# Loads, weight sums and query fills moved, and the last product cut in two, in a TensorE-bound transformer block

## The chip, the cores and the metric

The kernel runs on one core of a Trainium2 chip. The metric is the time of one execution on the device, in microseconds (us). Each kernel was run several times, in rounds together with the kernel before on the same chip; one run of each was also recorded by the hardware profiler. PE is the TensorE, DVE the VectorE, ACT the ScalarE, SP the engine that issues most DMAs. A "hole" below is a stretch in which PE starts no matmul.

## The reference

For x of 2048 rows and 1024 columns (bf16), in short:

```python
def A(x):                              # linear attention, 32 heads of 32
    q, k, v = split(x @ wqkv)
    pq, pk = phi(q), phi(k)            # phi(t) = t+1 if t > 0 else exp(t); plus 1e-6
    kv = einsum("bhsd,bhse->bhde", pk, v);  z = sum_s pk
    return ((pq @ kv) / (pq . z + 1e-6)) @ wo
def B(x):                              # MLP over the rows, F = 3584
    u = gelu(layernorm(x).T @ w1 + b1)
    return (u @ w2 + b2).T
h  = x + A(layernorm(x))
h2 = h + B(layernorm(h))
```

## The kernel before

The program has four stretches: a head, in which rows of x are normalised, transposed and multiplied by the key weights, tile by tile (a tile is 128 rows; "unit (i,c)" is tile i times key or value block c of 512 columns); the V and K runs, in which key and value projections of two tiles at a time are done with seven instead of eight block products (Strassen's scheme in Winograd's form, parts p1 to p7); attention; and the MLP, again with seven products (m1 to m7). Query projections ("fills") are put between parts of the runs where PE would wait.

The loads of the head: the first block of the key weights goes in two halves on the queue of ACT, all else on that of SP.

```python
xs = {0: load_x(0, True)}              # x0 in two halves, one on each queue
for k0 in (0, hk):
    pin(nc.scalar.dma_start(wkv[:, k0:k0+hk, 0:CW], wqkv_v[:, k0:k0+hk, D:D+CW]))   # key block 1
for i in range(1, 4):
    xs[i] = load_x(i)
for c in range(1, 2 * NDC):            # key block 2, value blocks 1 and 2
    nc.sync.dma_start(wkv[:, :, c*CW:(c+1)*CW], wqkv_v[:, :, D+c*CW:D+(c+1)*CW])
    ...                                # x4, x5; later the query weights
```

The end of the head and the first V run. `pin` keeps program order on an engine. `ln_stats` is DVE work (statistics of a tile); `ln_finish` is Ln and Exp on ACT, a normalisation on DVE and a transposing DMA. `w_sums` and `x_sums` are DVE work: four sums of 1.2 us (128x2048), four of 0.42 us (128x512). A fill is eight matmuls, then Exp and Relu on ACT and two DVE instructions.

```python
proj_unit(3, 0, pin)
ln_stats(G0)                           # G0 = 4
proj_unit(2, 1, pin)
load_biases(trp)
ln_finish(G0)
proj_unit(3, 1, pin)
...                                    # value units of tiles 0 and 1, w_sums(vmov, ..), x_sums(1)
v1 = VRun(1)
v1.p1(); q_fill(); kv_accum(0); kv_accum(1)
v1.p6(); v1.p2()
w_sums(kmov, 0)
q_fill()
ln_stats(G0 + 2)
v1.p5()
q_fill()
ln_finish(G0 + 2)
load_next(2 * G0)
v1.p7()
w_sums(kmov, 1)
q_fill()
x_sums(2)
...                                    # K run 2: p1, (p3, p4 of v1), p6, ...
```

In a run, p1 makes `psA` and ACT copies it to `psB`; p6 accumulates into `psB`, which lies in one of two PSUM slots that the fills use too. While `psB` lives there is one slot for fills, so a fill waits until the Relu of the fill before has read its slot.

The last product of the MLP, and the way its result leaves:

```python
def evac(sh, dh, ps):                  # DVE, then the store
    nc.vector.scalar_tensor_tensor(ot[sh][:, c], ps[:], b2_sb[...], hr[sh][:, c], ALU.add, ALU.add)
    nc.sync.dma_start(o_dram[...], ot[sh][:, c])
def m7(self):
    self.mm(7, self.X, False, True)    # 14 matmuls of 128x512
    self.evac(0, 0, self.X)
...
pend.m7()                              # end of the program
```

## Time and profile before

Before: 581.24 us, median of 3 runs (581.16 to 581.6). The profiled run was the one of 581.6 us.

| | value | view |
|---|---|---|
| span | 579.9 us | page |
| PE busy | 569.9 us, 98% | page |
| start to start of 128x512 matmuls, everywhere but in the warm-up | 0.216 us | timeline |
| waits of PE, all listed | 4.9 us | waits |
| start of the last product to the end | 6.9 us | timeline |

The chain of waits of the kernel before, by engine (first line of that part of the page):

```profile
PE 96%; DMA 1%; DVE 1%; ACT 0%; issue 0%; ACTq 0%; DVEq 0%
```

Who PE waited for in the kernel before (total us, times, longest):

```profile
PE acc_t L422 <- DMA wkv<-in_A_wqkv_dram: 2.0, 2, 1.3
PE acc_t L93 <- DVE warm L85: 1.2, 1, 1.2
PE psB L498 <- DVE xs L484: 0.9, 1, 0.9
PE acc_t L753 <- ACT r_sb L161: 0.6, 2, 0.3
PE tp L666 <- DVE xn L401: 0.2, 1, 0.2
```

So a change of order can win at most some 4 us, and a part of the tail. Where the waits lie, from the timeline of PE (start, length, what; in brackets the idle time and what ended it). The length of a matmul group includes the drain of the last one, so a hole is better read from start to start.

```profile
7.93 1.02 PE L422 MATMUL acc_t<-wkv,xnT 128*128 128x512 bf16 x4 [1.34 <-DMA wkv<-in_A_wqkv_dram]
8.96 0.72 PE L666 MATMUL tp<-ident,xn 128*128 128x128 bf16 x8
10.39 2.75 PE L422 MATMUL acc_t<-wkv,xnT 128*128 128x512 bf16 x12 [0.70 <-DMA wkv<-in_A_wqkv_dram]
...
34.91 1.02 PE L498 MATMUL psB<-wo_sb,xs 128*128 128x512 f16 x4
...
39.70 1.89 PE L753 MATMUL acc_t<-xnT,wq_sb 128*128 128x512 bf16 x8 [0.31 <-ACT r_sb L161]
41.42 1.03 PE L498 MATMUL psC<-wo_sb,xs 128*128 128x512 f16 x4
42.76 1.89 PE L753 MATMUL acc_t<-xnT,wq_sb 128*128 128x512 bf16 x7 [0.31 <-ACT r_sb L161]
...
48.15 1.04 PE L498 MATMUL psB<-pqT,xs 128*128 128x512 f16 x4 [0.92 <-DVE xs L484]
...
572.97 3.19 PE L228 MATMUL psX<-gO,sa 128*128 128x512 f16 x14
```

The first and the third line begin with the two halves of unit (0,0), which wait for the two halves of the key weights; the second is the transposes of tile 1. The line at 34.91 is p6 of the first V run. The two at 39.70 and 42.76 are fills that wait for the Relu (`r_sb`) of the fill before. The one at 48.15 is p6 of K run 2, which waits for its x sums. The last is the last product.

### The profile page before, as it was taken

The page shows a single profiled execution, that of the slowest core. Times are in us where ns is not written, and L with a number is a line of the kernel's source. Part 1 is how long each engine was busy: PE and PEld are TensorE (multiplying, and loading weights), DVE is VectorE, ACT ScalarE, POOL GpSimd, SP SyncE. Part 2 cuts the span into 40 slices and gives each one's busy share as a digit, 9 for nine tenths or more (in the row PEclk, how much of TensorE's full clock was granted, in tenths as well). Part 3 has the DMA queues.
Part 4 walks back from the last instruction along what each step waited for, and adds up shares of the span by engine and source line. Part 5 has one row for each costly group of instructions (what it writes and reads, how often), then busy time and mean ns, then how long its engine had stood idle before and what let it go on. Part 6 is the DMA issues. An engine that isn't in the chain of part 4 may idle for free.

```text
span 579.9 us, 7451 instructions
## 1 busy us (share of the span) xinstructions
PE 569.9 (98%) x2817; PEld 266.4 (46%) x2840; DVE 386.0 (67%) x751; ACT 212.5 (37%) x432; POOL 1.8 (0%) x8
## 2 busy tenths in 40 slices
PE   7999999999999999999999999999999999999997
PEld 3444444454555444444444444444444444444443
DVE  6788888546667889876666766667765456456542
ACT  4756777765667777342222322223000000000000
POOL 1000000000000000000000000000000000000000
PEclk9999999999999999999999999999999999999999
DMA  9933333019637952152224322203966446531101
GB/s 304 353 69 74 73 74 55 19 44 316 96 73 152 292 174 92 56 145 72 73 72 118 100 74 72 73 0 96 226 205 162 125 114 172 137 90 46 36 28 36
DMA packets 109667, 66.55 MB, mean 115 GB/s; under 512 B 31666, under 2 KB 101568, under 8 KB 109632
## 3 DMA queue, kind: packets, MB, share of 16 engines
q1 hardware_dynamic: 108368, 64.89, 42.7%
q10 hardware_dynamic: 1200, 1.18, 0.6%
q8 instruction: 22, 0.36, 0.3%
q14 instruction: 13, 0.11, 0.1%
q0 software_dynamic: 64, 0.01, 0.0%
HBM read 50.34 MB, written 8.39 MB: 101 GB/s over the span
## 4 chain that ended last, share of the span: by engine, by line
PE 96%; DMA 1%; DVE 1%; ACT 0%; issue 0%; ACTq 0%; DVEq 0%
PE psX L228 17%; PE psZ L228 17%; PE psW L228 17%; PE acc_t L902 9%; PE acc_t L753 9%; PE psY L228 8%; PE psB L498 4%; PE psA L498 4%; PE psC L498 4%; PE acc_t L422 3%; PE psE L498 2%; DMA wkv<-in_A_wqkv_dram 1%; PE nd_ps L853 1%; PE kvps_462 L451 1%; PE kvps_463 L451 0%; DVE pqT L472 0%
## 5 line engine op out<-in xcount | busy, mean ns | idle before, releaser
L228 PEld LDWEIGHTS <-sa 128*128 128x128 f16 x1120 | 109.6, 98 | 132.2
L223 DVE TENSOR_TENSOR sa<-w1p 128x1024 f16<-128x1024 bf16 x70 | 48.0, 685 | 20.0 <-PE psX L228 12.4
L753 PE MATMUL acc_t<-xnT,wq_sb 128*128 128x512 bf16 x247 | 57.4, 379 | 1.0 <-ACT r_sb L161 0.6
L902 PE MATMUL acc_t<-wo_sb,pqT 128*128 128x512 bf16 x250 | 55.7, 379 | 0.3
L223 DVE TENSOR_TENSOR sa<-w2p 128x1792 f16<-128x1792 bf16 x40 | 43.4, 1084 | 10.1 <-PE psW L228 7.6
L902 PEld LDWEIGHTS <-pqT 128*128 128x128 bf16 x256 | 24.8, 98 | 29.0
L753 PEld LDWEIGHTS <-wq_sb 128*128 128x128 bf16 x256 | 24.5, 98 | 28.4 <-issue 1.2
L164 DVE TENSOR_SCALAR e_sb<-e_sb 128x512 bf16<-128x512 bf16 x64 | 18.5, 290 | 27.3 <-ACT e_sb L160 26.7
L264 DVE TENSOR_TENSOR tt<-psW,dd 128x512 f32<-128x512 f32 x22 | 15.2, 692 | 29.2 <-PE psW L228 29.2
L228 PEld LDWEIGHTS <-w1p 128*128 128x128 bf16 x224 | 21.9, 98 | 26.4
L228 PEld LDWEIGHTS <-w2p 128*128 128x128 bf16 x224 | 21.9, 98 | 26.4
L160 ACT ACTIVATE e_sb<-acc_t 128x512 bf16<-128x512 f32 x40 | 23.9, 599 | 26.9 <-PE acc_t L753 23.7
L259 DVE TENSOR_TENSOR psY<-psX,dd 128x512 f32<-128x512 f32 x22 | 15.4, 699 | 27.5 <-PE psX L228 27.5
L498 PEld LDWEIGHTS <-xs 128*128 128x128 f16 x208 | 20.0, 98 | 24.1 <-DVE xs L484 2.3
L269 DVE TENSOR_TENSOR tt<-tt,psZ 128x512 f32<-128x512 f32 x22 | 15.1, 688 | 18.0 <-PE psZ L228 17.9
L228 PE MATMUL psZ<-hT_2226,w1p 128*128 128x512 f16 x112 | 26.8, 379 | 0.0
L228 PE MATMUL psW<-hE,sa 128*128 128x512 f16 x112 | 26.6, 379 | 0.0
L228 PE MATMUL psX<-hT_2225,sa 128*128 128x512 f16 x112 | 26.6, 379 | 0.0
L498 PE MATMUL psA<-wkv,xnT 128*128 128x512 bf16 x99 | 26.3, 379 | 0.3
L228 PE MATMUL psZ<-hO,sa 128*128 128x512 f16 x112 | 26.5, 379 | 0.0
L228 PE MATMUL psW<-hT_2227,w1p 128*128 128x512 f16 x112 | 26.5, 379 | 0.0
L228 PE MATMUL psY<-hE,sa 128*128 128x512 f16 x112 | 26.5, 379 | 0.0
(256 smaller groups left out, 839.1 us busy)
## 6 DMA issues: line engine op xcount, KB each, us to landing
w1p<-in_B_w_dram SPq DMA_DIRECT2D x14, 1024.0 KB, 5.8
w2p<-in_B_w_dram SPq DMA_DIRECT2D x8, 1792.0 KB, 8.5
xr<-in_A_x_dram SPq DMA_DIRECT2D x16, 256.0 KB, 3.4
x_sb<-in_A_x_dram SPq DMA_DIRECT2D x15, 256.0 KB, 3.7
wkv<-in_A_wqkv_dram SPq DMA_DIRECT2D x3, 1024.0 KB, 10.4
wq_sb<-in_A_wqkv_dram SPq DMA_DIRECT2D x2, 1024.0 KB, 11.4
wo_sb<-in_A_wo_dram SPq DMA_DIRECT2D x2, 1024.0 KB, 6.6
wkv<-in_A_wqkv_dram ACTq DMA_DIRECT2D x2, 512.0 KB, 7.6
```

The costliest lines, as they stand in the source:

```text
L160: pin(nc.scalar.activation(e_sb[:], src, ACT.Exp))
L164: pin(nc.vector.tensor_scalar(e_sb[:], e_sb[:], 1.0, PHI_EPS, ALU.min, ALU.add))
L223: return nc.vector.tensor_tensor(t, a, b, op)
L228: nc.tensor.matmul(ps[:], lhsT=sa[:, k, :], rhs=mv(k), start=(start and k == 0), stop=(stop and k == self.nk - 1), skip_group_check=True,)
L259: nc.vector.tensor_tensor(self.Y[:], self.X[:], self.d[:], ALU.add)
L264: nc.vector.tensor_tensor(self.t[:], self.W[:], self.d[:], ALU.add)
L269: nc.vector.tensor_tensor(self.t[:], self.t[:], self.Z[:], ALU.subtract)
L422: mm = nc.tensor.matmul(pp[:, 0:CW], lhsT=xnT[:, kt, i * P:(i + 1) * P], rhs=wkv[:, kt, c * CW:(c + 1) * CW], start=(kt == 0), stop=(kt == ...
L451: pin(nc.tensor.matmul(kv_ps[b][:, sl, :], lhsT=pks[i % NPK][:, j * P:(j + 1) * P], rhs=vaugs[i % NVA][:, j, :], start=False, stop=(i == N ...
L498: pin(nc.tensor.matmul(ps[:], lhsT=lhs[:, k, :], rhs=rhs[:, k, :], start=(start and k == 0), stop=(k == hk2 - 1), skip_group_check=True,))
L753: nc.tensor.matmul(qp[:, 0:SW], lhsT=wq_sb[:, kt, j * P:(j + 1) * P], rhs=xnT[:, kt, u * SW:(u + 1) * SW], start=(kt == 0), stop=(kt == ND ...
L902: nc.tensor.matmul(ap_[:, 0:CW], lhsT=pqT[:, j, i * P:(i + 1) * P], rhs=wo_sb[:, j, dc * CW:(dc + 1) * CW], start=(j == 0 and not SEED_RES ...
```

## The change

Its intent: bring the key weights in before x2 and x3; do two of the four key weight sums early; put p5 and p7 between the fills, so that no fill waits, and make the x sums of run 2 early; cut the last product in two column parts (384 and 128), so that the store of the first runs under the second. The number of fills before K run 2 drops from four to three; the fourth moves to the end of the runs.

```diff
-        def evac(sh, dh, ps):
+        def evac(sh, dh, ps, a=0, b=CW):            # only columns a to b
...
-        def m7(self):
-            self.mm(7, self.X, False, True)
-            self.evac(0, 0, self.X)
+        def m7(self, cuts=(0, CW)):
+            for a, b in zip(cuts, cuts[1:]):
+                self.mm(7, self.X, False, True, cols=slice(a, b))
+                self.evac(0, 0, self.X, a, b)
...
             xs = {0: load_x(0, True)}
+            xs[1] = load_x(1)
             for k0 in (0, hk):
-                pin(nc.scalar.dma_start(wkv[:, k0:k0 + hk, 0:CW], wqkv_v[:, k0:k0 + hk, D:D + CW]))
+                nc.sync.dma_start(wkv[:, k0:k0 + hk, 0:CW], wqkv_v[:, k0:k0 + hk, D:D + CW])
...
-            for i in range(1, 4):
+            for i in range(2, 4):
                 xs[i] = load_x(i)
...
                 if i == 2:
                     phis[0][1]()
                     phis[1][1]()
+                    w_sums(kmov, slice(0, 1))
...
             proj_unit(3, 0, pin)
+            w_sums(kmov, slice(1, 2))
             ln_stats(G0)
...
             v1.p2()
-            w_sums(kmov, 0)
+            w_sums(kmov, slice(2, 4))
             q_fill()
+            x_sums(2)
             ln_stats(G0 + 2)
             v1.p5()
-            q_fill()
+            v1.p7()
             ln_finish(G0 + 2)
             load_next(2 * G0)
-            v1.p7()
-            w_sums(kmov, 1)
             q_fill()
-            x_sums(2)
...
-            for n in range(2):
+            for n in range(3):
                 q_fill()
...
-    pend.m7()
+    pend.m7((0, CW - P, CW))
```

More of the change, by code (lines that the diff above doesn't have):

```diff
@@ L188, in prefetch @@
                 ot.append(outp.tile([P, D], BF16, tag=f"ot{a}", name=f"ot{a}"))
-        def evac(sh, dh, ps):
+        def evac(sh, dh, ps, a=0, b=CW):
             i = 2 * p + sh
-            c = slice(dh * CW, (dh + 1) * CW)
-            nc.vector.scalar_tensor_tensor(ot[sh][:, c], ps[:], b2_sb[:, i:i + 1], hr[sh][:, c], ALU.add, ALU.add)
+            c = slice(dh * CW + a, dh * CW + b)
+            nc.vector.scalar_tensor_tensor(ot[sh][:, c], ps[:, a:b], b2_sb[:, i:i + 1], hr[sh][:, c], ALU.add, ALU.add)
             nc.sync.dma_start(o_dram[i * P:(i + 1) * P, c], ot[sh][:, c])
@@ L223, in asum, with mm @@
             return nc.vector.tensor_tensor(t, a, b, op)
-        def mm(self, m, ps, start, stop, ks=None):
+        def mm(self, m, ps, start, stop, ks=None, cols=slice(0, CW)):
             sa, mv = self.sa[m], self.mov[m]
@@ L228, in mm @@
                 nc.tensor.matmul(
-                    ps[:],
+                    ps[:, cols],
                     lhsT=sa[:, k, :],
-                    rhs=mv(k),
+                    rhs=mv(k)[:, cols],
                     start=(start and k == 0),
@@ L320, in w1_evac, with evac @@
     def w1_evac(p):
-        def evac(fh, dh, ps):
+        def evac(fh, dh, ps, *cut):
             dst = (gE if fh == 0 else gO)[:, p, dh * CW:(dh + 1) * CW]
@@ L470, in w_sums @@
                 (b11, b12, b21, b22), (t1, t2, t3, t4) = mov
-                for out, a, b in ((t1, b12, b11), (t2, b22, t1), (t3, b22, b12), (t4, b21, t2))[2 * part:2 * part + 2]:
+                for out, a, b in ((t1, b12, b11), (t2, b22, t1), (t3, b22, b12), (t4, b21, t2))[part]:
                     pin(nc.vector.tensor_tensor(out, a, b, ALU.subtract))
@@ L738 @@
             proj_unit(0, NDC, pin)
-            w_sums(vmov, 0)
+            w_sums(vmov, slice(0, 2))
             proj_unit(0, NDC + 1, pin)
@@ L742 @@
             proj_unit(1, NDC, pin)
-            w_sums(vmov, 1)
+            w_sums(vmov, slice(2, 4))
             proj_unit(1, NDC + 1, pin)
```

## The prediction

> **What bounds it now.** TensorE. The chain of waits is 96% PE, the page shows PE busy 98% of 579.9 us, and a 128x512 matmul starts every 0.216 us wherever PE runs. Only PE gaps and the tail can be won. The timeline shows them (start to start): 1.3 us at 6.6 us (first key unit waits for the key weights, queued on ACT); 0.7 us at 9.7 us (their second half, landing at 10.35); 0.48 us at 39.2 and at 42.3 us (each query fill waits until the fill before has freed its PSUM slot); 1.1 us at 47.1 us (K run 2 waits for its x sums, behind two 1.2 us key weight sums on DVE); 3.9 us after the last matmul.
>
> **Key weights behind x0, x1.** In the DMA records both queues share one stream of about 340 GB/s, so today x2 and x3 travel beside the key weights; the Trainium skill, "DMA: Bandwidth & Descriptors", section "Queues, rings and completion order", says too that an engine alternates between queues. Queued first, the halves should land near 6 and 8 us. The second transposes still wait for DVE (8.96 us), so the first hole only shifts; the second closes (0.7 us). Then unit (0,1) needs the next key block: last landing 13.03 us today, used at 13.42, its bytes not moved earlier. I expect a new DMA wait; net 0.25 us (0 to 0.7).
>
> **Key sums early.** Two 1.2 us sums enter DVE between 17 and 23 us, where it idles for little more than one of them; it is packed from 22.4 to 34.8 us. The first V run's s1, s2 end at 34.13, PE needs them at 34.91. DVE falls 1.1 us behind PE, the slack is 0.7: a new wait of 0.4 us at psB of the first V run.
>
> **Fills respaced.** p5 and p7 now stand between fills (1.73 us, against the 1.3 us that Exp and Relu need after one): both 0.48 us holes go, and the hole at the x sums too: 2.05 us. But ACT now meets Ln/Exp of tile 6, which stand before the third fill's Exp/Relu and K run 2's copy to psB, only after DVE finished x sums and statistics. From the end of fill 2 I sum 7.0 us of measured steps to K run 2's p6, against 6.0 us of PE work: a new hole of 1.0 us there. Net 1.05 us. The moved fill runs at the phase's end without a wait.
>
> **Last product in 384+128 columns.** Meant to overlap evacuation and store. But in the built program the second part's first matmul waits for the first part's evacuation: same PSUM bank. (The skill, "PSUM — Partial Sum Buffer", section "Terms", calls two engines in one bank at once an error; no run here shows it.) Estimate, from 129-column matmuls at 0.058 us and 0.75 us for a 512-column evacuation: 2.27 + 0.2 + 0.6 + 0.06 + 0.85 + 0.2 + 0.3 + 2.65 to the end = 7.1 us, against 6.93 now: 0.2 us lost.
>
> **Sum.** 0.25 - 0.4 + 1.05 - 0.2 = 0.7 us gained: 580.5 us, range 579.6 to 581.4. Faster by over 2%: 0.01; within 2%: 0.98; slower: 0.01.
>
> **Shows right or wrong:** no PE wait before the second half of unit (0,0); a DMA wait near 13 us; V run 1's p6 waiting for xs; no waits between fills; K run 2's p6 waiting for ACT; PE idle 0.9 us between the last product's parts.
>
> **Could be wrong:** key block 2 landing later; DVE's lag absorbed; a shorter ACT chain; a tail that gains.

## The result and the profile after

Changed kernel: 580.85 us, median of 6 runs (580.36 to 581.29); before: 581.25 us (581.16 to 581.6, 6 runs). The ratio of the fast runs is 0.9992, with a 95% interval of 0.9979 to 1.0005: the same. (Ratios in this text are the mean time of one kernel's fast runs over that of the other's of the same rounds, so not quite the ratio of the medians quoted.) The outputs are correct. In these rounds the runs of the changed kernel lie wider apart than those of before: 0.93 us against 0.44. In the later rounds the kernel before scattered as much or more (fast runs 580.89 to 582.54, 580.87 to 582.09 and 581.02 to 582.75 us), so a wider scatter of the changed kernel is not shown.

The profiled run took 580.46 us (span 578.7 us). Who PE waited for in the changed kernel (its line numbers are up to four higher):

```profile
PE tp L668 <- DVE xn L402: 2.0, 2, 1.0
PE acc_t L93 <- DVE warm L85: 1.2, 1, 1.2
PE psX L228 <- DVE ot_5119 L193: 0.7, 1, 0.7
PE psB L499 <- ACT psB L512: 0.5, 1, 0.5
PE acc_t L423 <- ACT r_sb L161: 0.4, 1, 0.4
PE acc_t L423 <- ACT xnT L678: 0.4, 1, 0.4
```

Of the old waits only the warm-up's and that of the transposes (`tp`, for DVE's normalisation) are left. The second is 2.0 us here and 0.2 above, and the one for `xnT` (0.4 us) is not in the list above; but a second trace of the kernel before, shown below, has both at the same 2.0 and 0.4 us, so the change did not bring them. The other three are new. The timeline of PE:

```profile
7.13 1.04 PE L423 MATMUL acc_t<-wkv,xnT 128*128 128x512 bf16 x4 [0.35 <-ACT xnT L678]
9.15 0.72 PE L668 MATMUL tp<-ident,xn 128*128 128x128 bf16 x8 [0.98 <-DVE xn L402]
9.71 2.75 PE L423 MATMUL acc_t<-wkv,xnT 128*128 128x512 bf16 x12
12.29 0.61 PE L668 MATMUL tp<-ident,xn 128*128 128x128 bf16 x8
12.79 3.61 PE L423 MATMUL acc_t<-wkv,xnT 128*128 128x512 bf16 x15
...
26.08 5.34 PE L423 MATMUL acc_t<-wkv,xnT 128*128 128x512 bf16 x24 [0.36 <-ACT r_sb L161]
...
34.79 1.02 PE L499 MATMUL psB<-wo_sb,xs 128*128 128x512 f16 x4
...
45.08 1.02 PE L499 MATMUL psB<-pqT,xs 128*128 128x512 f16 x4 [0.55 <-ACT psB L512]
...
571.61 2.44 PE L228 MATMUL psX<-gO,sa 128*128 128x384 f16 x14
574.76 0.94 PE L228 MATMUL psX<-gO,sa 128*128 128x128 f16 x14 [0.71 <-DVE ot_5119 L193]
```

The fills wait no more. The hole before p6 of K run 2 is now from 44.37 (four matmuls of 0.216 us after 43.51, where p4 starts) to 45.08, 0.7 us, ended by ACT's copy to `psB`. A new hole of 0.5 us stands before 26.08 us. And between the parts of the last product PE stands idle: 14 matmuls of 0.162 us (three quarters of 0.216) after 571.61 end at 573.88, the next starts at 574.76, 0.88 us later, when DVE has evacuated the first part.

The new hole at 26 us comes from DVE by way of ACT. The timeline of ACT in the changed kernel there:

```profile
22.56 0.59 ACT L161 ACTIVATE r_sb<-acc_t 128x512 bf16<-128x512 f32 x1
24.53 0.29 ACT L398 ACTIVATE lnv<-mv,eps_ln 128x1 f32<-128x1 f32 x1 [1.38 <-DVE mv L395]
24.86 0.20 ACT L399 ACTIVATE rstd<-lnv 128x1 f32<-128x1 f32 x1
24.96 0.58 ACT L160 ACTIVATE e_sb<-acc_t 128x512 bf16<-128x512 f32 x1
25.44 0.59 ACT L161 ACTIVATE r_sb<-acc_t 128x512 bf16<-128x512 f32 x1
```

ACT waits 1.38 us with Ln of tile 4 for the statistics (`mv`), which stand on DVE behind the second early key sum; the Exp and Relu of unit (3,1) stand behind it on ACT, although their data is there, and PE needs the PSUM slot that this Relu frees.

### The profile page after: what moved, and what is told of

It reads as the page before. It is cut to its first block, busy times and chain, and to the rows that moved or that the text cites. A ratio compares the mean times of both kernels' runs of the same rounds, so it can differ in the third digit from the quotient of the medians.

```text
span 578.7 us, 7486 instructions
## 1 busy us (share of the span) xinstructions
PE 569.4 (98%) x2832; PEld 267.2 (46%) x2854; DVE 385.7 (67%) x752; ACT 211.9 (37%) x432; POOL 1.8 (0%) x8
## 4 chain that ended last, share of the span: by engine, by line
PE 96%; DVE 2%; ACT 1%; issue 0%; DMA 0%
PE psX L228 17%; PE psW L228 17%; PE psZ L228 17%; PE acc_t L904 9%; PE acc_t L757 9%; PE psY L228 8%; PE psB L499 4%; PE psA L499 4%; PE psC L499 4%; PE acc_t L423 3%; PE psE L499 2%; PE nd_ps L855 1%; DVE st L392 1%; PE kvps_464 L452 1%; PE kvps_465 L452 0%
## 5 line engine op out<-in xcount | busy, mean ns | idle before, releaser
L228 PE MATMUL psX<-hO,sa 128*128 128x512 f16 x112 | 26.5, 379 | 0.0
```

The lines of the kernel that those rows point to most:

```text
L228: nc.tensor.matmul(ps[:, cols], lhsT=sa[:, k, :], rhs=mv(k)[:, cols], start=(start and k == 0), stop=(stop and k == self.nk - 1), skip_gro ...
```

## The experiments

Twelve kernels ran, one of them the kernel before again, all with correct outputs. They ran on two chips, so each is best compared by its ratio to the kernel before in the same rounds; the changed kernel has 0.9992. One run of the kernel before took 1877.52 us and counts as slow; it is in no ratio.

### The tail: last product whole

```diff
-    pend.m7((0, CW - P, CW))
+    pend.m7()
```

> The changed kernel with the last product in one piece again. My theory: the second part waits for the first part's evacuation, so the cut costs; without it the span after the start of the last product goes from 7.09 us back to about 6.93, and the time falls by 0.1 to 0.2 us. Rival, the intent of the cut: it hides most of an evacuation, so without it the time rises by 0.3 to 0.5 us.

Measured: 580.86 us (580.41 to 581.78, 5 runs), ratio to before 0.9992 (0.9979 to 1.0005). From the start of the last product to the end: 6.86 us in its trace, 7.07 in that of the changed kernel (571.61 to 578.68), 6.88 in that of before (572.97 to 579.86). The cut costs 0.2 us in the traces; the medians, with their scatter, don't resolve that. The rival's 0.3 to 0.5 us gain is ruled out by the traces.

### The tail: two PSUM banks

```diff
+            # last pair only: psX for columns 0..383, a second psX tile for 384..511;
+            # m1, the two DVE adds into psX, m7 and evac work on (tile, a, b) in turn
+        def m7(self):
+            for ps, a, b in self.parts():
+                self.mm(7, ps, False, True, cols=slice(a, b))
+                self.evac(0, 0, ps, a, b)
```

> The changed kernel, with the last pair's accumulator in two PSUM banks (384 and 128 columns), so that the second part need not wait for the evacuation of the first; the first product of that pair is cut in the same places. My theory (the shared bank makes the wait): no PE idle time between the two parts, and about 6.4 us from the start of the last product to the end instead of 7.09, so 0.6 us less than the changed kernel. Rival (128-column matmuls or the second small store are what costs): the tail stays within 0.2 us of 7.09.

Measured: 580.16 us (579.43 to 580.73), ratio 0.9978 (0.9965 to 0.9991). The tail takes 6.18 us, 0.9 less than in the changed kernel and 0.7 less than before. Its timeline of PE:

```profile
572.16 3.22 PE L230 MATMUL psX<-gO,sa 128*128 128x384 f16 x28
```

All 28 matmuls are one uninterrupted group: the 128-column part is no burden in itself. So the wait came with the shared bank, and the intent of the cut was sound and its form was not. (This version also makes two tiles of one; no run tells the shared tile from the shared bank.) The Trainium skill, "PSUM — Partial Sum Buffer", section "Terms", says that TensorE writing and VectorE reading one bank at once is an error; the built program accordingly had a wait for the evacuation at the first matmul of the second part, and no run here tried without.

### The loads: new order alone

```diff
# on the kernel before
+            xs[1] = load_x(1)
             for k0 in (0, hk):
-                pin(nc.scalar.dma_start(...))
+                nc.sync.dma_start(...)
-            for i in range(1, 4):
+            for i in range(2, 4):
```

> The kernel before with the new order of loads alone (key weights behind x0 and x1 on one queue). My theory: the wait of 0.7 us before the second half of unit (0,0) goes, PE runs 0.6 to 0.7 us earlier from there to the first V run, DVE has slack there, so the kernel is 0.4 to 0.7 us faster than before (580.5 to 580.9). Rival: the gain is taken back by x2 or key block 2 landing later, or by the x sums, and the time stays within 0.2 us of before.

Measured: 581.27 us (581.06 to 581.45), ratio 0.9999 (0.9985 to 1.0013). The rival was right: no gain.

### The kernel before, a second look

> The kernel before, unchanged, for a second trace. The first one came from a run of 581.6 us, 0.4 above the usual 581.2, and one of the 16 landings of every load after about 7 us came some 1.07 us after the other 15. My theory: that late engine differs from run to run, and the 0.7 us hole before the second half of unit (0,0), which the prediction counted as the prize of the new queue order, is largely the late engine's doing. Then a run near 581.1 shows last landings within 0.3 us of the 15th and a hole of 0.2 us or less there. Rival: the hole is that of the two queues sharing the engines, and it is again 0.6 to 0.8 us.

Measured: 580.92 us (one run), span 579.1 us. The timeline of PE in this second trace of the kernel before:

```profile
7.09 1.04 PE L422 MATMUL acc_t<-wkv,xnT 128*128 128x512 bf16 x4 [0.36 <-ACT xnT L676]
9.11 0.72 PE L666 MATMUL tp<-ident,xn 128*128 128x128 bf16 x8 [0.98 <-DVE xn L401]
9.66 2.75 PE L422 MATMUL acc_t<-wkv,xnT 128*128 128x512 bf16 x12
12.25 0.61 PE L666 MATMUL tp<-ident,xn 128*128 128x128 bf16 x8
12.70 1.67 PE L422 MATMUL acc_t<-wkv,xnT 128*128 128x512 bf16 x6
```

The two DMA waits of the first trace (1.34 and 0.70 us) are not there. They were not a property of the kernel but of that run. Every load is spread over 16 DMA engines and posts 16 landings; the time of the 15th and of the last, from the records of the traces (us):

```
                          before, 1st trace   before, 2nd trace   changed kernel
key block 1, 1st half       6.93 /  7.79        5.71 /  5.74        6.67 /  6.70
key block 1, 2nd half       9.52 / 10.35        9.30 /  9.32        8.38 /  8.39
key block 2                11.96 / 13.03       11.59 / 11.61       12.74 / 12.75
```

In the first trace one landing is 0.8 to 1.1 us behind the other 15. In the second it is not. The new order brings the second half in earlier (8.4 us), but PE cannot use it before 9.7 us, since it comes to it only after the second transposes, which wait for DVE. And it brings the first half and key block 2 in later by 1 us each. The first half now has x1 in front of it. Key block 2 has the same bytes in front of it in both orders; there the reason is the rate. Busy time of each engine and, last, the GB/s of all DMA between 5.0 and 6.5 us in the second trace of before, then in the trace with the new order alone:

```profile
5.00:6.50 1.50, 0.52 (x8) 0.39 (x8) 1.24 (x3) 0.53 (x3) 0.00 (x0) 1.00 1.08 381
```

```profile
5.00:6.50 1.50, 1.02 (x7) 0.28 (x6) 1.35 (x4) 0.50 (x2) 0.00 (x0) 1.00 0.76 238
```

In the four traces with the loads on two queues that stretch shows 342 to 381 GB/s; in the ten with one queue 181 to 351. Why the single queue is slow there was not tested.

### Key block 2 in two halves

```diff
             for c in range(1, 2 * NDC):
-                nc.sync.dma_start(wkv[:, :, ...], wqkv_v[:, :, ...])
+                # c == 1: two DMAs, k 0..3 and 4..7
```

> The changed kernel with key block 2 loaded in two halves, so that the first four matmuls of unit (0,1) need only the first half. In the profiled run of the changed kernel the whole block's last landing was at 12.75 us and PE used it at 12.79. My theory for the wider scatter of its times (580.36 to 581.29, against 581.16 to 581.6 of before): in some runs one of the 16 landings comes up to 1 us later and PE waits. Then the halves bring the median to about 580.4 and the scatter below 0.5 us. Rival (scatter comes from elsewhere, such as the granted clock): median and scatter stay as they are, 580.8 and 0.9 us.

Measured: 581.51 us (580.48 to 582.14), ratio 1.0000 (0.9985 to 1.0015): slower and more scattered, against the theory. But the five runs fall into two groups: 580.48 and 580.56 with a mean granted clock of 1.000, and 581.51, 582.09 and 582.14 with 0.996 or 0.997. The profiled run is of the second kind. Two lines of its timeline of PE:

```profile
8.03 1.09 PE L423 MATMUL acc_t<-wkv,xnT 128*128 128x512 bf16 x4 [1.17 <-DMA wkv<-in_A_wqkv_dram]
...
10.06 3.85 PE L423 MATMUL acc_t<-wkv,xnT 128*128 128x512 bf16 x12
```

Twelve matmuls take 3.85 us instead of 2.75. The two stretches of 3.41 us around it, with the trace's own clock records as borders (busy us of PE first, granted clock third from the end):

```profile
5.44:8.86 3.42, 1.72 (x13) 0.77 (x12) 2.26 (x7) 1.27 (x4) 0.00 (x0) 1.00 0.95 317
8.86:12.27 3.41, 3.30 (x15) 1.67 (x15) 2.23 (x6) 1.71 (x5) 0.00 (x0) 0.50 1.08 370
```

The clock ran at half speed for one stretch of 3.41 us, after one in which PE was busy for 1.72 us only, since the first half of the key weights landed late (7.89 us). The Trainium skill, "TensorE: Matmul & The Clock Gate", section "Part 1: The HAM clock gate (the "warmup" mystery)", tells of a window of 3413 ns, after an idle one of which the clock falls to half; the trace agrees with the length. So my theory named the wrong consequence of late loads.

### Matmuls without use in the holes of the head

```diff
             transpose_in(0)
+            keep_warm(0, 2)        # two 128x512 matmuls on zeros, overwritten later
...
             k_parts(0, 0, lo_k)
+            keep_warm(1, 3)
```

> The kernel with key block 2 in halves, plus five 128x512 matmuls without use: two before and three after the first half of unit (0,0), in holes of PE. Three of five runs of the halves without them had a mean clock of 0.996 or 0.997 and were 0.9 to 1.6 us slower than the other two; the profiled one shows the clock at half speed for 3.4 us from 8.9 us on, after a stretch in which PE stood idle much of the time. My theory: PE idleness in the head lets the clock fall; with the holes filled no run has a mean clock below 0.998 and the median falls from 581.5 to about 580.5. Rival: the drops come at random; then one to four of five runs show them again.

Measured: 580.84 us (580.73 to 583.08), ratio 1.0000 (0.9985 to 1.0014). Four runs have a clock of 0.999 or 1.000 and lie within 0.36 us; one has 0.997 and took 583.08. The median fell by 0.67 us, but "no drop" failed: one of five against three of five decides nothing.

### Key weights later still, without and with such matmuls

```diff
# late_weights, on the changed kernel
-            xs[1] = load_x(1)
+            for i in range(1, 4):          # x1, x2, x3, then the key weights
+                xs[i] = load_x(i)
# late_weights_warm: also
             transpose_in(0)
+            keep_warm(0, 8)
```

> The changed kernel with the key weights queued behind x3 as well, so that their first half lands near 8 us or later and PE stands idle longer after the first transposes. The two traces with a clock drop in the head (block2_halves, sums_late) are those whose first half landed latest, at 7.7 to 7.9 us; those with 7.5 or earlier have none. Theory: idleness of PE in the head drops the clock. Then the profiled run shows half speed for 3.4 us near 8 to 12 us, most runs have a mean clock of 0.997 or less, and the time is 1.5 to 3 us over the changed kernel. Rival (drops are random): at most one run in three has one, and the time is about 1 us over the changed kernel, for the later weights alone.

> The same with eight 128x512 matmuls without use (1.7 us at full clock) in the hole before the first key unit. Theory of idleness: no drop of the clock in any run, mean clock 0.999 or 1.0, and a time 1.0 to 1.5 us below late_weights. Rival (drops are random, or come from the load stream): the same share of drops as in late_weights, and no less time.

Measured: without, 581.94 us (580.64 to 582.39, 4 runs), three of four with a clock of 0.997 (581.61, 582.39, 582.26), one with 1.000 (580.64). With, 580.68 us (580.49 to 580.96), all four with 1.000. Ratios to before 1.0005 (0.9989 to 1.0020) and 0.9981 (0.9967 to 0.9994). In both traces the first half is used at the same time, 8.54 and 8.53 us, so the loads are alike; only PE's idleness differs. That speaks for idleness and against chance, with few runs. The profiled run without the extra matmuls happened to be the one with the full clock, so the picture of the drop that the expectation promised is missing; and the time is 1.1 us over the changed kernel's median, less than the 1.5 to 3 expected. The trace also shows that the later load as such costs little: its PE timeline reaches the last product at 571.79 us, the changed kernel's at 571.61. I had expected 1 us from it. Nor does a late landing alone bring the drop: in the first trace of before the first half landed at 7.79 us and the clock stayed up.

### Ln and Exp behind the work they held up

```diff
-            ln_finish(G0)
             proj_unit(3, 1, pin)
+            ln_finish(G0)
...
             v1.p7()
-            ln_finish(G0 + 2)
-            load_next(2 * G0)
             q_fill()
+            ln_finish(G0 + 2)
+            load_next(2 * G0)
```

> The changed kernel with the Ln and Exp of tile 4 behind the last key unit and those of tile 6 behind the third fill, on ACT; no work is removed. My theory: in the changed kernel ACT stands at these two small instructions until DVE has the statistics, and holds back the freeing of a PSUM slot (hole of 0.5 us at 25.6 us) and the copy to psB of K run 2 (hole of 0.7 us at 44.4 us). With them behind, both holes go and the time falls by 0.7 to 1.2 us, less up to 0.3 us if p6 of the first V run then waits for its x sums. Rival: DVE itself is late, not the order on ACT; then both holes stay within 0.2 us of what they were.

Measured: 579.93 us (579.69 to 580.53), ratio 0.9977 (0.9964 to 0.9989): 0.9 us below the changed kernel's median. Its timeline of PE at the two places:

```profile
22.50 8.81 PE L423 MATMUL acc_t<-wkv,xnT 128*128 128x512 bf16 x39
...
33.73 1.11 PE L452 MATMUL kvps<-vaug,pk 128*128 128x129 bf16 x16
34.96 1.04 PE L499 MATMUL psB<-wo_sb,xs 128*128 128x512 f16 x4
...
43.69 1.02 PE L499 MATMUL psC<-wo_sb,xnT 128*128 128x512 f16 x4
44.55 1.03 PE L499 MATMUL psB<-pqT,xs 128*128 128x512 f16 x4
```

The group at 22.50 is not broken, and p6 of K run 2 follows p4 by 0.86 us, which is four matmuls: both holes are gone. So ACT's order made them, and DVE's lateness alone did not. In return p6 of V run 1 starts 1.23 us after the 16 small matmuls in front of it (33.73 to 34.96) instead of 0.94 in the changed kernel (33.85 to 34.79): a hole of 0.3 us that ends with a DVE x sum (34.48 to 34.90), as the last clause of the expectation had it.

### Key sums where they were

```diff
-                    w_sums(kmov, slice(0, 1))
-            w_sums(kmov, slice(1, 2))
-            w_sums(kmov, slice(2, 4))
+            w_sums(kmov, slice(0, 4))      # before the second fill
```

> The changed kernel with all four key weight sums where two and two stood before (in the first V run, before the second fill). My theory: the early sums cost a hole of 0.5 us at 25.6 us (DVE late, so ACT late), which then goes; but four sums of 1.2 us before the second fill's Exp push the x sums of run 2 and tile 6's statistics back by 2.4 us, and the hole before p6 of K run 2 grows from 0.7 to 2.5 to 3 us. So 1.3 to 2.0 us slower than the changed kernel, about 582.4. Rival (early sums buy nothing): within 0.3 us of the changed kernel.

Measured: 582.06 us (581.07 to 582.86), ratio 1.0010 (0.9996 to 1.0023). Two of five runs have a clock of 0.997, the profiled one among them; the other three took 581.07, 581.23 and 582.86. In the trace the hole at 26 us is gone, as expected. Before p6 of K run 2 stands a hole of 0.7 us as in the changed kernel, and before p4 of the first V run a new one of 1.1 us (start to start 0.93 and 1.30 us, less 0.216), ended by a DVE add: 1.8 us in all, not 2.5 to 3. From p6 of V run 1 to p6 of K run 2 it takes 11.29 us against 10.29. So in the traces the early sums win 1.0 us there and lose 0.5 at 26 us; in the times, under the scatter and the clock, that can't be told apart from the rest.

### Loads as before, the rest changed

```diff
-            xs[1] = load_x(1)              # and the key weights back on the ACT queue
```

> The changed kernel with the loads as they were before: key block 1 on the ACT queue, x1 to x3 on the other. Theory after the first eight runs: the new order brings nothing (the new order alone ran at 0.9999 of before), since the single queue moves only some 240 GB/s between 5.0 and 6.5 us, where the two together move 380; it makes the first half of the key weights land at 6.5 to 7.9 us instead of 5.7, key block 2 at 12.7 to 13.3 instead of 11.6, and with them the scatter and the clock drops. Then the old order is 0.2 to 0.6 us faster than the changed kernel (580.2 to 580.6) and its runs lie within 0.4 us, none with a mean clock under 0.998. Rival: the order is neutral and the scatter has another cause; then 580.8 with a scatter of 0.9 us.

Measured: 580.69 us (580.42 to 581.68), ratio 0.9984 (0.9972 to 0.9997). By the ratios that is 0.5 us less than the changed kernel, by the medians 0.16 us, and the intervals overlap: a gain of the old order is not shown. No clock under 0.998, as expected; but the scatter is 1.26 us, which the theory ruled out. On that chip the kernel before scattered too (581.02 to 582.75, nine runs), so a part of the scatter belongs to neither the queue order nor the clock. It stays open.

### The parts that paid, together

Loads on two queues as before, fills and key sums as changed, `ln_finish` of tiles 4 and 6 later, the last product in two banks.

> The parts that the runs speak for, together: loads on two queues as before, fills respaced and key sums early as in the changed kernel, Ln and Exp of tiles 4 and 6 behind the unit and the fill, the last product in two PSUM banks. From 581.2: 2.0 us of holes between the fills and at the x sums less 0.4 us lost again at the first V run, and 0.4 to 0.6 us of the tail: about 579.1, range 578.7 to 579.5, scatter within 0.4 us. Rival: the gains overlap (earlier work waits at the next place), then 579.6 or more.

Measured: 578.78 us (578.65 to 579.89), ratio 0.9953 (0.9938 to 0.9967), before in the same rounds 581.81 us. Faster than before by 0.5%, clear of the noise, and every run is below every run of the changed kernel (which ran in other rounds). What PE still waits for in it by the list of waits (span 576.9 us), all of it in the first 10 us:

```profile
PE tp L681 <- DVE xn L416: 1.6, 2, 1.0
PE acc_t L93 <- DVE warm L85: 1.2, 1, 1.2
PE acc_t L437 <- ACT xnT L691: 0.4, 1, 0.4
```

A hole too short for that list is left: p6 of V run 1 starts 1.20 us after the small matmuls (33.33 to 34.53) instead of 0.94. One run of the five, 579.89 us at full clock, is unexplained; with it the scatter is 1.24 us, not within the 0.4 expected.

## Why the prediction was right or wrong

The predicted time, 580.5 us, with 579.6 to 581.4 around it, holds the measured 580.85; "within 2%" was right. The range also holds the time of before, 581.25, so this alone says little. The terms behind it, against the traces. All columns are starts of groups in the timelines of PE and the ends of the spans, in us.

| | before, 1st trace | before, 2nd trace | changed |
|---|---|---|---|
| p6 of V run 1 starts | 34.91 | 34.19 | 34.79 |
| from there to p6 of K run 2 | 13.24 | 13.24 | 10.29 |
| from there to the last product | 524.82 | 524.82 | 526.53 |
| from there to the end | 6.88 | 6.89 | 7.07 |

Against the second trace, which stands for the usual run of 581.1 us, the changed kernel loses 0.60 us in the head, wins 2.95 in the runs, gives back 1.71 later (the moved fill, eight matmuls) and loses 0.18 in the tail: 0.46 us gained, near the 0.40 of the medians. Against the first trace it would be 1.18 us. The gain did not vanish anywhere; the first trace overstated what there was to gain.

- **Key weights behind x0, x1** ("the second closes (0.7 us)", net 0.25): the step that failed. The holes of that trace were made by one late landing in 16. A second trace has none, and the new order alone gave a ratio of 0.9999. The order is worth nothing here, because the second transposes wait for DVE anyway, and it lands key block 2 about 1 us later than a usual run of before. The "new DMA wait near 13 us" was not in the trace of the changed kernel, by 0.04 us (last landing 12.75, use 12.79); it was in that with two banks, where the landing was at 13.29 and PE waited 0.28 us by the profile.
- **Key sums early** ("a new wait of 0.4 us at psB of the first V run"): the lag of DVE was right, the place was not. It showed at 26 us as a hole of 0.5 us, by way of ACT's Ln of tile 4. I had reckoned the effect of late statistics on ACT for tile 6 and missed the same thing for tile 4. After that hole p6 found its x sums ready. With ACT's order changed (ln_both_later) the hole at 26 us goes and 0.3 us appears at p6, where the prediction had put 0.4.
- **Fills respaced** (net 1.05, new hole of 1.0): right in kind. 2.95 less 1.73 of moved work is 1.22 us; the new hole is 0.7 us, ended by ACT's copy to `psB`, as said. The chain from the fill to the copy was over-estimated by 0.3 us. The moved fill ran without a wait.
- **Last product cut** (0.2 lost, PE idle 0.9 us): 0.18 to 0.21 us lost, idle 0.88 us. With the parts in two banks the idle time is gone.

In sum the prediction had 0.25 - 0.4 + 1.05 - 0.2 = 0.7 us; against the usual run of before the traces have -0.1 (unit (0,1) starts at 12.79 instead of 12.70), -0.5, +1.2 and -0.2, that is 0.4 to 0.5 us. The range covered the difference.

What was not predicted: the changed head can let the clock fall for 3.41 us. One of six runs of the changed kernel had a mean clock of 0.997, and it was the slowest, 581.29 us. Over all rounds a mean clock of 0.996 or 0.997 stands in 11 of 40 runs with the loads on one queue and no extra matmuls (6 of the 11 in block2_halves and late_weights, none in the 5 of the new order alone), and in 1 of the 39 fast runs with two queues whose clock is on record (581.94 us, the kernel before). The first clock record lies at 4.3 to 7.0 us in the 14 traces, so a stretch of 3.41 us covers another part of the head in each run; that may be why only some runs drop, but it was not tested. The rest of the scatter, of both kernels, is open.

## What to carry to other kernels

Take a second trace of the kernel before when the prize is below 1 us: here 0.7 us of it belonged to one run. When an engine gets work earlier, follow its lateness through the other in-order engines: a 0.3 us Ln that waits for statistics held back a PSUM slot that was ready. Here a product cut in column parts overlapped with its evacuation once the parts lay in two PSUM tiles in two banks (6.18 us for the tail), and not in one (7.07, and 6.88 uncut).

## What the Trainium skill lacked or had wrong

- "DMA: Bandwidth & Descriptors", section "Issuing engines are not separate DMA queues", says that issuing from several engines at once saves only the sequencer's time. Here, between 5.0 and 6.5 us, four traces with the loads on two queues show 342 to 381 GB/s, and ten with one queue 181 to 351; key block 2 landed at 11.6 to 12.0 us in three of the four, and at 12.7 to 13.6 us in the one-queue traces that load it whole. The cause was not tested.
- The same page, section "Why a DMA increments its semaphore by 16 and not by 1", tells that the engines of one DMA finish independently, not by how much: the last of 16 landings came up to 1.6 us after the 15th (6.28 and 7.89 us, block2_halves), in one run and not in another of the same kernel (1.07 and 0.02 us for key block 2 in the two traces of before).
- "TensorE: Matmul & The Clock Gate", section "Part 1: The HAM clock gate (the "warmup" mystery)", lets the clock fall after an idle window; how busy a window may be and still count as idle, the page does not say. In block2_halves it fell after a stretch in which PE was busy for 1.72 of 3.42 us, in sums_late after 1.53 of 3.41; it did not after 1.76 (the new queue order alone), 1.89 (late_weights) and 2.07 (the changed kernel). So a window about half busy was not safe here. Busy time alone doesn't draw the line: at the end of the program the clock fell after 1.57 us (old_queue, 573.63 to 577.04) and not after 1.67 (tail_whole, 573.36 to 576.77).
